# Inverting only the diagonal halves of the triangular matrices of a chunked recurrence

## The chip, the cores and the metric

The kernel runs on one core of a Trainium2 chip. The metric is the device time of one execution in microseconds. Its engines are TensorE (PE), VectorE (DVE), ScalarE (ACT), GpSimd (POOL), and SyncE (SP), which issues all of this kernel's transfers. TensorE's clock has two levels, 1.2 and 2.4 GHz; the profile gives the granted clock of a stretch as a share of the higher.

## What is computed

For 32 heads (4 batches of 8) with a state of 40x40 and 768 steps:

```python
for t in range(S):
    y[:, :, t] = einsum('bhd,bhde->bhe', rt, state)
    Sa = einsum('bhde,bhe->bhd', state, at)
    state = state * wt[:, :, None, :] - einsum('bhd,bhe->bhde', Sa, bt)
    state = state + einsum('bhd,bhe->bhde', vt, kt)
```

Its output, as 3072 tokens of 320, goes through two feed-forward nets (320 to 1536 gated, 320 to 1024 with a softmax and a norm). All is float32.

## The kernel before

**Chunks and slots.** The 768 steps are cut into 24 chunks of CH = 32. Within a chunk the vectors Sa of the 32 steps depend on each other through a triangular 32x32 matrix per head, so with T, the inverse of (identity less that matrix), all come at once: u = T rn, where rn is what the state at the chunk's start gives. Two chunks form a group n (12 groups), with 64 matrices. The work runs in slots, one for a chunk and half of the heads: `slot(s)`, s from -6 to 48; state-carrying slots are 0 to 47. The time of a slot is read here from one copy rn (line 298) to the next.

**The places of a slot.** A slot has ten places, `work`, in the order in which every engine gets its instructions (each engine runs its own in that order, and waits where it must): 0 `m_r` (matmuls pr, copy rn) and `m_st` (the state turned, pst); 1 and 2 `m_ruv` (matmuls pruv, then two masks RL on VectorE); 3 `m_u` (matmuls pu = T rn, on ScalarE four copies into Z and one us); 4 and 5 `products` of chunk half s + 9 (pABK, copies abn, a store of abn to DRAM `ab`); 6 `m_y` (pY); 7 `m_state` (pS; VectorE adds into the next Z, in two slots of four with a product with PE, line 332); 8 `m_ut` and `natural` (put, pBK). After each place `fill` puts other work in: from slot 6 on one unit of the first net on TensorE at four of the places (`UNITS`; a gate or value of 8 matmuls, or an output of 6), pieces of a weight conversion (tile `flat`, lines 584 to 603), and a share of the list `back`.

**The solve.** `back` holds the solve of group n, by forward substitution on VectorE. Partitions are the 64 matrices times two halves (even and odd rows), so that one instruction serves all. `t_iter(n, j)`, j from 0 to 30, multiplies column j of the rows so far with row j of M into `tmp` (line 260) and adds it to TT (line 264); both are split in two where VectorE is to shorten a dependence, and half of group 1 runs on GpSimd. Group n is solved in the slots s = 4n - 5 + k, k = 0 to 3 (in slots 17 and 21, k is 2), by the table `SOLVE`; in k = 0 twelve empty places come first. `decay` (two scans, lines 154 and 161, a check, line 144, a reciprocal and a copy) stands at the head of `back` in the slots of k = 2 and k = 3.

**Transfers.** `t_load` brings M (two copies, 64 rows of 4 KB each) at place 6 of the slot before k = 0, once the last store of abn has landed. `t_store` writes TT to DRAM (`tt`) in rows of 32 numbers, after k = 3; for group 0 after slot -3. `t_fetch` brings TB for a chunk at place 4 of odd slots. SP issues in the same order and waits at an instruction whose data isn't there.

**PSUM.** Four buffers go round for pr, pst, pruv, pu, pABK, pS, put and pBK.

Of the kernel before, what the change touches and what calls it, by code (L numbers as in the profile page):

```python
# [24 lines left out]
CH = 32  # L25
# [8 lines left out]
SOLVE = (0, 0, 13, 26, 31), (0, 0, 11, 21, 31), (0, 6, 15, 23, 31)  # L34
T1 = 2
STORE = 5
# [6 lines left out]
UNITS = (2, 5, 7, 9)  # L43
# [25 lines left out]
class Attention:  # L69
    def __init__(self, tc, ctx, d, xT, abd, ttd, bad, ident, zero, memory):  # L70
# [21 lines left out]
        self.tmp = [cp.tile([128, 160], F32, name=f"tmp{i}") for i in range(3)]  # L92
# [19 lines left out]
        for t in self.Z + self.UV:  # L112
            nc.gpsimd.memset(t, 0.0)
# [84 lines left out]
    def products(self, i):  # L198
# [40 lines left out]
    def eye(self, n):  # L239
        TT = self.T[n] = self.sb.tile([128, CH // 2, CH], F32, tag="TT", name=f"TT{n}", bufs=2)  # L240
        self.nc.sync.dma_start(out=TT.rearrange("p j t -> p (j t)"), in_=self.d["ceye"])
        return TT

    def t_load(self, n):
        nc = self.nc
        M = self.sb.tile([128, CH, CH], F32, tag="M", name=f"M{n}", bufs=2)
        twice(nc, M.rearrange("p j t -> p (j t)"), self.abd[n])
        self.T[n] = (M, self.T.get(n) or self.eye(n))

    def t_iter(self, n, j):  # L250

        nc = self.nc
        M, TT = self.T[n]
        k, m = CH - 1 - j, j // 2 + 1

        cut = min(m, T1) if n == 1 else m // 2 if m >= 4 and n in (0, 2) else 0
        parts = [(nc.vector, slice(0, cut), self.tmp[j % 2]), (nc.gpsimd if n == 1 else nc.vector, slice(cut, m), self.tmp[2 if n == 1 else j % 2])][cut == 0:1 + (cut < m)]

        def mult(eng, r, tmp):
            eng.tensor_tensor(out=tmp[:, 0:m * k].rearrange("p (c t) -> p c t", t=k)[:, r], in0=TT[:, r, j:j + 1].broadcast_to([128, r.stop - r.start, k]),  # L260
                              in1=M[:, j:j + 1, j + 1:CH].broadcast_to([128, r.stop - r.start, k]), op=ALU.mult)

        def add(eng, r, tmp):
            eng.tensor_tensor(out=TT[:, r, j + 1:CH], in0=TT[:, r, j + 1:CH], in1=tmp[:, 0:m * k].rearrange("p (c t) -> p c t", t=k)[:, r], op=ALU.add)  # L264
        return [lambda x=x, f=f: f(*x) for f in (mult, add) for x in parts]

    def t_store(self, n):
        M, TT = self.T.pop(n)
        for par in range(2):
            self.nc.sync.dma_start(out=self.ttd[n].rearrange("p (c two t) -> p two c t", two=2, t=CH)[:, par], in_=TT[64 * par:64 * par + 64])  # L270
# [11 lines left out]
    def t_fetch(self, c):  # L282
        n, k = divmod(c, SS)
        self.nc.sync.dma_start(out=self.TB[c % 2], in_=self.ttd[n].rearrange("(k h q) (j t) -> k (q j) h t", k=SS, q=4, t=CH)[k])

    def m_r(self, i):
# [1212 lines left out]
```

## Time and profile before

| | us |
|---|---|
| median of 3 runs | 1196.82 (1193.41 to 1199.75) |
| the profiled execution | 1195.06 |
| its span in the profile | 1193.3 |
| VectorE busy | 888.6 (74%) |
| TensorE busy (matmuls) | 1019.1 (85%) |
| ScalarE, GpSimd busy | 582.7, 484.9 |
| granted clock, mean | 0.931 |

The profile is of one execution, whose own time is 1.8 us more than its span. Busy time is an average over stages: before slot 0 (to 73 us), slots 0 to 5 with the conversion of the first net's weights (to 178.5), slots 6 to 37 (to 606.7), slots 38 to 47 (to 705.7), and the rest of the nets. Busy shares of TensorE include pipelined overlap; how far it is full is best seen where one matmul group follows the next without a gap.

### The profile page before, as it was taken

The numbers are of one execution on the slowest core, as the hardware profiler recorded it, in microseconds if no ns is written. First come the engines' busy times: TensorE is split into PE (matmuls) and PEld (weight loads), VectorE is DVE, ScalarE is ACT, GpSimd is POOL, SyncE is SP. The second block draws the span as 40 slices with busy tenths as digits, with TensorE's granted clock in tenths as the row PEclk, the third lists the DMA queues.
The fourth block names the chain that finished last, engine by engine and source line by source line (L and its number), as shares of the span: only waits on it lengthen the run. The fifth ranks groups of instructions, "written<-read, shape, count | busy, mean of one in ns | idle before, by whom it ended". The sixth has DMA issues, their size and how long they took to land.

```text
span 1193.3 us, 32044 instructions
## 1 busy us (share of the span) xinstructions
PE 1019.1 (85%) x12677; PEld 874.1 (73%) x12710; DVE 888.6 (74%) x2132; ACT 582.7 (49%) x1503; POOL 484.9 (41%) x545
## 2 busy tenths in 40 slices
PE   5536778786978888787989998999999998999997
PEld 2313547675867777676878888888888876888897
DVE  8969999999998999999999644554311249776673
ACT  4244545565656555655666754434322234454453
POOL 7548644455554546554543322222222211222232
PEclk8668977898989988998999999999999999999999
DMA  6464655566667575665655734422110000000001
GB/s 179 127 146 124 149 140 128 143 163 165 157 182 185 144 190 146 189 155 149 176 146 152 193 91 121 135 80 83 29 65 1 1 1 1 23 18 23 17 23 37
DMA packets 187951, 130.53 MB, mean 109 GB/s; under 512 B 107216, under 2 KB 167376, under 8 KB 187792
## 3 DMA queue, kind: packets, MB, share of 16 engines
q1 hardware_dynamic: 187792, 128.38, 40.8%
q8 instruction: 103, 1.69, 0.6%
q14 instruction: 56, 0.46, 0.1%
HBM read 104.19 MB, written 24.15 MB: 108 GB/s over the span
## 4 chain that ended last, share of the span: by engine, by line
PE 47%; DVE 36%; DMA 7%; issue 4%; ACT 2%; SPq 2%; POOL 2%; DVEq 0%; ACTq 0%; POOLq 0%
PE hid L816 20%; DVE tmp L260 8%; DVE TT L264 8%; DVE Z L329 3%; PE three L1182 2%; PE three L1185 2%; PE three L1183 2%; DVE RL L370 2%; DVE Q L154 2%; PE two L849 2%; PE two L1169 2%; PE two L851 2%; DVE G L161 1%; PE two L850 1%; PE one L816 1%
## 5 line engine op out<-in xcount | busy, mean ns | idle before, releaser
L264 DVE TENSOR_TENSOR TT<-TT,tmp 128x30 f32<-128x30 f32 (+38 forms) x422 | 160.6, 389 | 8.2
L816 PE MATMUL hid<-l_x,l_w 128*128 128x512 f32 x672 | 160.3, 391 | 0.0
L260 DVE TENSOR_TENSOR tmp<-TT,M 128x30 f32<-128x30 f32 (+38 forms) x422 | 148.6, 361 | 11.8 <-DMA TT<-in_ceye_dram 6.8
L816 PEld LDWEIGHTS hid<-l_x,l_w 128*128 128x128 f32 x672 | 124.4, 188 | 24.1 <-issue 0.2
L533 POOL TENSOR_TENSOR l_x<-l_plain,l_x 128x512 fp32r<-128x512 f32 x43 | 55.6, 1292 | 185.2 <-ACT l_x L532 167.7
L816 PE MATMUL one<-b_tokens,b_w 128*128 128x256 f32 x816 | 127.3, 300 | 2.3 <-DVE b_plain L837 2.3
L837 DVE TENSOR_TENSOR l_plain<-hid,l_plain 128x512 f32<-128x512 f32 x43 | 29.7, 691 | 116.2 <-ACT l_plain L836 116.1
L816 PEld LDWEIGHTS one<-b_tokens,b_w 128*128 128x128 f32 x816 | 106.6, 195 | 8.1 <-DVE b_plain L837 2.6
L223 POOL TENSOR_TENSOR AT<-abn,mA 64x256 f32<-64x256 f32 x96 | 81.7, 851 | 66.5 <-ACT abn L218 60.8
L380 PE MATMUL pY<-RL,YR 128*40 128x32 f32 x1536 | 50.8, 213 | 62.5 <-DVE RL L370 61.9
L602 POOL TENSOR_TENSOR flat<-flat 128x224 f32<-128x224 f32 (+1 forms) x54 | 38.1, 706 | 151.3 <-DVE flat L601 68.5
L380 PEld LDWEIGHTS pY<-RL,YR 128*40 128x40 f32 x1536 | 41.8, 131 | 76.4 <-DVE RL L370 72.7
L816 PE MATMUL hid<-b_w,l_x 128*128 128x512 f32 x384 | 94.0, 397 | 2.6 <-DVE l_e L1141 2.6
L532 ACT ACTIVATE b_tokens<-b_plain 128x256 fp32r<-128x256 f32 (+1 forms) x70 | 33.5, 487 | 105.5 <-DVE b_plain L837 95.7
L816 PEld LDWEIGHTS hid<-b_w,l_x 128*128 128x128 f32 x384 | 70.9, 188 | 19.0 <-DVE l_e L1141 3.6
L533 POOL TENSOR_TENSOR b_tokens<-b_plain,b_tokens 128x256 fp32r<-128x256 f32 x58 | 44.7, 770 | 91.5 <-ACT b_tokens L532 86.4
L206 PE MATMUL pABK<-AT,BK 128*64 128x64 f32 x768 | 62.1, 238 | 22.2 <-POOL BK L196 21.3
L836 ACT ACTIVATE l_plain<-hid 128x512 f32<-128x512 f32 x43 | 25.6, 597 | 110.4 <-PE hid L816 110.4
L206 PEld LDWEIGHTS pABK<-AT,BK 128*64 128x64 f32 x768 | 54.1, 150 | 33.8 <-POOL BK L196 23.5
L195 POOL TENSOR_TENSOR AT<-AT,G 40x256 f32<-40x256 f32 x90 | 70.9, 787 | 13.5 <-DMA AT<-in_LA_dram 10.3
L312 ACT ACTIVATE Z<-pu 32x160 f32<-32x160 f32 x192 | 56.3, 293 | 32.3 <-PE pu L309 29.8
L1176 POOL TENSOR_TENSOR l_w<-l_e,l_w 128x1024 fp32r<-128x1024 f32 x12 | 28.8, 2402 | 88.7 <-ACT l_e L1137 51.1
(247 smaller groups left out, 2639.9 us busy)
## 6 DMA issues: line engine op xcount, KB each, us to landing
AT<-in_LA_dram SPq DMA_DIRECT2D x48, 256.0 KB
RL<-in_RS_dram SPq DMA_DIRECT2D x24, 512.0 KB
LB<-in_LB_dram SPq DMA_DIRECT2D x46, 208.0 KB
Z<-in_VN_dram SPq DMA_DIRECT2D x48, 160.0 KB
M<-ab SPq DMA_DIRECT2D x24, 256.0 KB
UV<-in_VT_dram SPq DMA_DIRECT2D x24, 208.0 KB
G<-in_LW_dram SPq DMA_DIRECT2D x22, 214.5 KB
flat<-in_moe_w_out_dram SPq DMA_DIRECT2D x21, 224.0 KB
```

Source lines behind the costliest of these rows:

```text
L195: eng.tensor_tensor(out=at[SROW[g], g], in0=at[SROW[g], g], in1=G[SROW[g]], op=ALU.mult)
L206: yield lambda m=m: nc.tensor.matmul(ps[0:64, m * 64:m * 64 + 64], lhsT=bkt[:, m].rearrange("p s t -> p (s t)"), rhs=at[:, :, m, :], start ...
L223: nc.gpsimd.tensor_tensor(out=at[UROW[g], g].rearrange("p (a b) t -> p a b t", a=2), in0=abn[UROW[g], :, hs], in1=self.mA[UROW[g]].unsquee ...
L260: eng.tensor_tensor(out=tmp[:, 0:m * k].rearrange("p (c t) -> p c t", t=k)[:, r], in0=TT[:, r, j:j + 1].broadcast_to([128, r.stop - r.star ...
L264: eng.tensor_tensor(out=TT[:, r, j + 1:CH], in0=TT[:, r, j + 1:CH], in1=tmp[:, 0:m * k].rearrange("p (c t) -> p c t", t=k)[:, r], op=ALU.add)
L312: nc.scalar.activation(z[32 * q:32 * q + 32, hs, g, p * 4:p * 4 + 4, :], ps[32 * q:32 * q + 32, 0:160].rearrange("p (h d) -> p h d", d=40) ...
L329: nc.vector.tensor_tensor(out=o, in0=ps[SROW[g], 0:320].rearrange("p (n d) -> p n d", d=40), in1=z[SROW[g], hs, g], op=ALU.add)
L380: yield lambda m=m, g=g: nc.tensor.matmul(ps[SROW[g], m * CH:m * CH + CH], lhsT=yr[:, g, m, :], rhs=rl[:, hs, g, m, :], start=True, stop=True)
L532: nc.scalar.activation(h, src, AF.Copy)
L533: eng_l.tensor_tensor(out=l, in0=src, in1=h.bitcast(F32), op=ALU.subtract)
L602: lambda: self.eng.tensor_tensor(out=L, in0=L, in1=T, op=ALU.mult),
L816: nc.tensor.matmul(out, lhsT=a, rhs=b, start=n == 0, stop=n == 7)
```

## The change

VectorE inverts two 16x16 blocks of each matrix, the diagonal ones: partitions are now 64 matrices times two blocks, M is 16x16, and there are 15 steps of one multiplication and one addition, with no split and none on GpSimd. T = [[T1, 0], [corner, T2]] is never formed. Instead u comes in two passes: with the block-diagonal T, u1 = T rn; then the corner of the original matrix (LO, from `ab`) times u1's first half, plus rn, gives a new right side rm, and T rm is u. Line numbers of new code are those of the changed file.

```diff
-SOLVE = (0, 0, 13, 26, 31), (0, 0, 11, 21, 31), (0, 6, 15, 23, 31)
+HB = CH // 2
+SOLVE = (0, 5, 10, HB - 1)
-UNITS = (2, 5, 7, 9)
+UNITS = (3, 5, 7, 9)
...
     def t_load(self, n):
-        twice(nc, M.rearrange("p j t -> p (j t)"), self.abd[n])
+        for b in range(2):
+            r = slice(HB * b, HB * b + HB)
+            self.nc.sync.dma_start(out=M[64 * b:64 * b + 64], in_=self.abd[n].rearrange("m (j t) -> m j t", t=CH)[:, r, r])
...
     def t_iter(self, n, j):
-        k, m = CH - 1 - j, j // 2 + 1
...
+        k, m = HB - 1 - j, j + 1
+        D = TT[:, HB:].rearrange("p (c t) -> p c t", t=CH)
+        return [lambda: nc.vector.tensor_tensor(out=tmp, in0=D[:, 0:m, j:j + 1].broadcast_to([128, m, k]), in1=M[:, j:j + 1, j + 1:HB].broadcast_to([128, m, k]), op=ALU.mult),
+                lambda: nc.vector.tensor_tensor(out=D[:, 0:m, j + 1:HB], in0=D[:, 0:m, j + 1:HB], in1=tmp, op=ALU.add)]
...
     def t_store(self, n):
+        for b in range(2):
+            self.nc.sync.dma_start(out=self.ttd[n][:, HB * CH * b:HB * CH * (b + 1)], in_=TT[64 * b:64 * b + 64, HB - HB * b:HB - HB * b + HB * CH])
...
     def t_fetch(self, c):
+        self.nc.sync.dma_start(out=self.LO[c % 2][:, :, HB:CH], in_=steps(self.abd[n])[:, :, HB:CH])
...
+    def blocks(self, i, at):
+                self.nc.tensor.matmul(self.pr[r, at + x:at + x + 40], lhsT=self.TB[c % 2][r, hs * 4 + hh, :], rhs=self.rn[r, x:x + 40], start=True, stop=True)
+    def m_u1(self, i):
+        self.nc.scalar.activation(self.u1, self.blocks(i, 160), AF.Copy)
+    def m_u2(self, i):
+                self.nc.tensor.matmul(self.pr[32 * q:32 * q + 32, 320 + x:360 + x], lhsT=self.LO[c % 2][r, hs * 4 + hh, :], rhs=self.u1[r, x:x + 40], start=True, stop=True)
+        self.nc.vector.tensor_tensor(out=r, in0=self.pr[:, 320:480], in1=self.rn, op=ALU.add)
     def m_u(self, i):
-        ps = self.psum(f"pu{i}")
+        ps = self.blocks(i, 0)
...
-            if k == 0:
-                back += [None] * (12 if s >= 0 else 0)
-            steps = range(*SOLVE[min(n, 3) - 1][k:k + 2])
+            back += [f for j in range(*SOLVE[k:k + 2]) for f in self.t_iter(n, j)]
...
-            lambda: run(ruv, 4),
+            lambda: (run(ruv, 4), on and self.m_u1(s)),
             lambda: run(ruv),
-            lambda: on and self.m_u(s),
+            lambda: on and self.m_u2(s),
             lambda: run(prod, 4),
-            lambda: (run(prod), late and self.scaled(pi)),
+            lambda: (on and self.m_u(s), run(prod), late and self.scaled(pi)),
...
-        if 1 < n < NSS and k == 3:
+        if solve and k == 2:
             self.t_store(n)
-        if s == -3:
+        if s == -5:
             self.t_store(0)
             self.t_fetch(0)
```

All three steps write into pr's PSUM buffer, so pu is gone and pr is held to place 5. The seeds TT of groups 0 and 1 are loaded at the beginning.

TensorE, slot 21, from pruv to the state update. Before (pu is T rn, pABK the products, `one` a unit of the net):

```order
L366 MATMUL pruv_5365<-RL_183,UV_177 64x64 x8
L816 MATMUL one<-b_tokens,b_w 128x256 x8
L309 MATMUL pu_5391<-rn_5338,TB_185 32x40 x16
L206 MATMUL pABK_5418<-AT_159,BK_171 64x64 x8
L816 MATMUL one<-b_tokens,b_w 128x256 x8
L380 MATMUL pY_187<-RL_183,YR_179 40x32 x16
L326 MATMUL pS_5472<-Z_181,YR_180 40x40 x16
```

The same stretch of the changed kernel:

```order
L385 MATMUL pruv_5758<-RL_183,UV_177 64x64 x4
L305 MATMUL pr_5714<-rn_5731,TB_185 32x40 x16
L385 MATMUL pruv_5758<-RL_183,UV_177 64x64 x4
L319 MATMUL pr_5714<-u_21_5763,LO_188 32x40 x16
L831 MATMUL one<-b_tokens,b_w 128x256 x8
L207 MATMUL pABK_5824<-AT_159,BK_171 64x64 x4
L305 MATMUL pr_5714<-rm_5810,TB_185 32x40 x16
L207 MATMUL pABK_5824<-AT_159,BK_171 64x64 x4
L831 MATMUL one<-b_tokens,b_w 128x256 x8
L399 MATMUL pY_187<-RL_183,YR_180 40x32 x16
L345 MATMUL pS_5898<-Z_181,YR_180 40x40 x16
```

The one group pu has become three, each with an engine's work in between; the last of them stands between the halves of pABK.

VectorE, slot 21, from the head of the decay on (`rm` is the new right side, on which TensorE's second block product waits):

```order
L145 TENSOR_SCALAR G_0_5209<-G_0_5209 104x8x64
L155 SCALAR_TENSOR_TENSOR Q_193<-G_0_5209,d_152 104x528
L614 SCALAR_TENSOR_TENSOR flat<-flat 128x224
L159 RECIPROCAL d_152<-Q_193 104x8
L160 COPY PE_0_5710<-Q_193 104x8
L162 SCALAR_TENSOR_TENSOR G_0_5209<-G_0_5209,d_152 104x528
L389 TENSOR_TENSOR RL_183<-pruv_5758,mR 64x256 x2
L258 TENSOR_TENSOR tmp_190<-TT_4707,M_5144 128x55
L259 TENSOR_TENSOR TT_4707<-TT_4707,tmp_190 128x11x5
L321 TENSOR_TENSOR rm_5810<-pr_5714,rn_5731 128x160
```

The addition for rm is new; it stands behind the whole decay and the masks, where in the kernel before the masks RL were the last on which TensorE (pY) waited.

SP, around the store of T(0), of the changed kernel; before, it stood two slots later, behind the loads of UV and RL:

```order
L265 DMA tt_86<-TT_334 64x512 x2
L281 DMA TB_185<-tt_86 128x8x32
L282 DMA LO_188<-ab_74 128x8x16
L167 DMA AT_160<-in_LA_dram 128x512
L173 DMA LB_465<-in_LB_dram 104x512
L221 DMA ab_75<-abn_450 32x8x32 x4
```

The store, which waits for the solve, and the fetch behind it now come ahead of the loads of AT and LB and of a store of abn.

## Rows read from the trace of the kernel before

**Rows 1.** Stages (windows): us from:to, length, busy (instructions) per engine, PEclk, DMA share, GB/s.

```profile
73.00:178.50 105.50, 74.95 (x1155) 46.89 (x1171) 93.57 (x248) 50.01 (x149) 66.73 (x99) 0.84 0.57 143
178.50:606.70 428.20, 349.70 (x6702) 310.15 (x6714) 407.87 (x1002) 248.99 (x747) 227.68 (x275) 0.92 0.64 164
606.70:705.70 99.00, 94.21 (x1949) 84.82 (x1952) 75.19 (x219) 65.35 (x201) 33.69 (x49) 1.00 0.52 139
```

**Rows 2.** The same windows, instructions on the solve's tile tmp alone.

```profile
73.00:178.50 105.50, 39.76 (x131) 24.18 (x54) 0.84 0.57 143
178.50:606.70 428.20, 209.66 (x522) 0.00 (x0) 0.92 0.64 164
```

**Rows 3.** Windows of slots 15, 17 and 19, columns as in rows 1.

```profile
302.50:312.70 10.20, 10.16 (x215) 9.29 (x215) 9.06 (x26) 6.73 (x22) 5.76 (x8) 1.00 0.70 169
325.40:341.30 15.90, 12.69 (x221) 11.15 (x221) 15.48 (x32) 9.37 (x27) 13.21 (x14) 0.85 0.84 226
353.00:367.60 14.60, 12.12 (x231) 11.04 (x231) 11.64 (x35) 6.83 (x23) 5.48 (x8) 0.88 0.92 224
```

**Rows 4.** VectorE groups, 178.5 to 606.7: busy us, mean ns | idle before.

```profile
L329 DVE TENSOR_TENSOR Z<-pS,Z 40x320 f32<-40x320 f32 x64 | 31.0, 485 | 0.4
L370 DVE TENSOR_TENSOR RL<-pruv,mR 64x256 f32<-64x256 f32 x64 | 26.7, 418 | 2.0
L154 DVE TENSOR_TENSOR_SCAN Q<-G,d 104x528 f32<-104x528 f32 x15 | 25.2, 1680 | 0.5
L161 DVE TENSOR_TENSOR_SCAN G<-G,d 104x528 f32<-104x528 f32 x15 | 21.1, 1410 | 0.0
L332 DVE TENSOR_TENSOR Z<-Z,PE 40x320 f32<-40x320 f32 x32 | 19.2, 601 | 1.1
L597 DVE SCALAR_TENSOR_TENSOR flat<-flat 128x224 int32<-128x224 int32 x38 | 16.5, 435 | 2.4 <-ACT flat L584 2.1
...
L144 DVE TENSOR_SCALAR G<-G 104x512 f32<-104x512 f32 x15 | 7.0, 465 | 0.0
```

**Rows 5.** Timeline, slots 22 and 23: start us, us, engine, line, instruction.

```profile
404.17 0.23 DVE L260 TENSOR_TENSOR tmp<-TT,M 128x78 f32<-128x78 f32 x1
...
409.58 0.67 POOL L602 TENSOR_TENSOR flat<-flat 128x224 f32<-128x224 f32 x1 [3.23 <-DVE flat L601]
409.65 0.65 DVE L260 TENSOR_TENSOR tmp<-TT,M 128x30 f32<-128x30 f32 x1
...
410.33 0.19 DVE L264 TENSOR_TENSOR TT<-TT,tmp 128x30 f32<-128x30 f32 x1
```

**Rows 6.** Timeline of TensorE in slot 27.

```profile
467.37 0.49 PE L309 MATMUL pu<-rn,TB 32*32 32x40 f32 x32
467.79 1.15 PE L206 MATMUL pABK<-AT,BK 128*64 128x64 f32 x16
468.86 0.42 PE L849 MATMUL two<-b_w,b_tokens 128*128 128x320 f32 x1
...
469.94 0.81 PE L380 MATMUL pY<-RL,YR 128*40 128x32 f32 x32
470.68 0.81 PE L326 MATMUL pS<-Z,YR 64*40 64x40 f32 x32
471.41 1.20 PE L816 MATMUL one<-b_tokens,b_w 128*128 128x256 f32 x8
```

**Rows 7.** ScalarE groups, 178.5 to 606.7, the copy rn.

```profile
L298 ACT ACTIVATE rn<-pr 128x160 f32<-128x160 f32 x33 | 10.0, 302 | 0.8 <-PE pr L295 0.2
```

**Rows 8.** The chain that ended last, 606 to 626: start us, us, what.

```profile
613.87 2.75 DMA ab<-abn
...
617.21 4.80 DMA M<-ab
```

**Rows 9.** The same chain, 55 to 75.

```profile
59.97 2.93 DMA tt<-TT
```

**Rows 10.** Timeline of GpSimd, 22 to 78; in brackets its idle time before.

```profile
70.36 1.50 POOL L223 TENSOR_TENSOR AT<-abn,mA 64x256 f32<-64x256 f32 x2 [22.16 <-ACT abn L218]
```

More of the change, by code (lines that the diff above doesn't have):

```diff
@@ L111, in __init__ @@
             nc.vector.memset(t, 0.0)
-        for t in self.Z + self.UV:
+        for t in self.Z + self.UV + self.LO:
             nc.gpsimd.memset(t, 0.0)
@@ L253, in t_iter @@
         M, TT = self.T[n]
-        k, m = CH - 1 - j, j // 2 + 1
[L256 to L265, printed above, removed]
+        k, m = HB - 1 - j, j + 1
+        D = TT[:, HB:].rearrange("p (c t) -> p c t", t=CH)
+        tmp = self.tmp[j % 2][:, 0:m * k].rearrange("p (c t) -> p c t", t=k)
+        return [lambda: nc.vector.tensor_tensor(out=tmp, in0=D[:, 0:m, j:j + 1].broadcast_to([128, m, k]), in1=M[:, j:j + 1, j + 1:HB].broadcast_to([128, m, k]), op=ALU.mult),
+                lambda: nc.vector.tensor_tensor(out=D[:, 0:m, j + 1:HB], in0=D[:, 0:m, j + 1:HB], in1=tmp, op=ALU.add)]
     def t_store(self, n):
         M, TT = self.T.pop(n)
-        for par in range(2):
-            self.nc.sync.dma_start(out=self.ttd[n].rearrange("p (c two t) -> p two c t", two=2, t=CH)[:, par], in_=TT[64 * par:64 * par + 64])
+        for b in range(2):
+            self.nc.sync.dma_start(out=self.ttd[n][:, HB * CH * b:HB * CH * (b + 1)], in_=TT[64 * b:64 * b + 64, HB - HB * b:HB - HB * b + HB * CH])
     def z_load(self, c):
@@ L421, in begin @@
                 self.eye(0)
+                self.eye(1)
             run(self.products(i))
@@ L437, in slot @@
         n, k = divmod(s - (2 * SS + 1 - LOOK), 2 * SS)
-        if 0 < n < NSS:
-            if k == 0:
-                back += [None] * (12 if s >= 0 else 0)
+        solve = 0 < n < NSS and k < 3
+        if solve:
             if k == 2 and n + 1 < NSS:
                 self.eye(n + 1)
-            steps = range(*SOLVE[min(n, 3) - 1][k:k + 2])
-            back += [f for j in steps for f in self.t_iter(n, j)]
-        if s in range(-6, -2):
-            back += [f for j in range((s + 6) * 8, min((s + 7) * 8, CH - 1)) for f in self.t_iter(0, j)]
+            back += [f for j in range(*SOLVE[k:k + 2]) for f in self.t_iter(n, j)]
+        if s in (-6, -5):
+            back += [f for j in range((s + 6) * 8, min((s + 7) * 8, HB - 1)) for f in self.t_iter(0, j)]
         m, hs = pi // (2 * SS) + 1, (pi % (2 * SS)) // 2
@@ L475, in slot @@
                 self.t_load(pj // (2 * SS))
-            if s == 3 and p == STORE:
-                self.t_store(1)
             if p == 4 and s % 2 and 3 < s < NHS - 1:
```

52 lines of the change are left out of this document (30 added, 22 removed).

## The prediction

> **What bounds the kernel now.** I read the stages first, then VectorE alone, then single slots. By stage [rows 1] the last 488 us, the feed-forward part, hold nothing that the diff touches, so I let them stand. In slots 6 to 37 (178.5 to 606.7 us, 32 slots of 13.38 us) VectorE is busy 407.9 of 428.2 us, 95%, TensorE 349.7. Of VectorE's time 209.7 us are the triangular solve: 522 instructions of 0.40 us [rows 2]. So VectorE sets the pace, and half of its work there is what the change cuts. The single slots [rows 3] show the other limit: where few solve instructions fall (slot 15, from 302.5), TensorE is busy 10.16 of 10.2 us at full clock. In slot 17 (from 325.4), which also has a decay, VectorE is busy 15.48 of 15.9 us and TensorE's clock is 0.85.
>
> **The solve.** For one n there were 31 steps of a multiplication and an addition, two instructions each or, split, more: 522/8 = 65 per n in this stage. Now it is 15 steps, 30 instructions. The elements per partition fall from 2856 to 680 (the sum of rows times remaining columns over the steps), so from 92 a step to 45. The time of one instruction hardly depends on that: undisturbed it is 0.23 us at 78 elements and 0.19 at 30 [rows 5]. The 0.65 us at 409.65 is a wait: GpSimd's instruction runs from 409.58 to 410.25, VectorE's ends at 410.30. I take 0.40 less the 0.04 that the shorter work saves, 0.36 us; the bounds are 0.19 (never held up) and 0.65 (always). The Trainium skill, SBUF — State Buffer, section Who interferes with whom, says that an instruction of VectorE with two SBUF inputs and one of GpSimd that reads SBUF exclude each other for a whole instruction. Rows 5 agree to 0.05 us. By that rule the saving goes with the count of instructions, 65 to 30; were it to go with the elements, one would cost 0.40 x 45/92 = 0.20 us and the 30 would cost 6 us and not 10.8. So per four slots VectorE drops from 209.7/8 = 26.2 to 10.8 us, plus four additions for r. Such an addition (128x160, one input in PSUM) is not in the trace: at least 0.19, and I take the 0.42 of the mask RL (64x256 from PSUM) [rows 4]. VectorE's work per slot: (407.9 - 209.7)/32 + 10.8/4 + 0.42 = 9.3 us.
>
> **TensorE.** Two groups of 16 matmuls come in per slot, shaped like pu. From one start to the next, pu took 467.79 - 467.37 = 0.42 us [rows 6], so 0.84 us a slot. LO has half the rows; I don't credit that. Floor: 10.2 + 0.84 = 11.0 us, above VectorE's 9.3. So TensorE would set the pace wherever nothing else holds it up.
>
> **The new waits.** The step to u is now PE, ACT, PE, DVE, PE. The activation u1 costs 0.30 us, as rn does [rows 7]; on TensorE half of pruv, about 0.5 us, lies between it and the corner, so I cost it at nothing. ScalarE, busy 249 of 428 us [rows 1], has room for 0.3 more; if its queue holds another copy there, TensorE stands about as long. The addition for r is the dear one. It stands on VectorE behind everything from the state update Z on, and TensorE's second block product stands before pY and pS, on which the next Z waits. That is a loop: VectorE from Z to r, then TensorE from the block product to pS. TensorE's part by [rows 6]: pu 0.42, half of pABK 0.53, a unit 1.08, pY 0.74, pS 0.73, together 3.5; I add 0.2 for hand-overs.
> - Slots with a decay and a solve (k = 2): Z 2 x 0.49, RL 2 x 0.42, scans 1.68 and 1.41, check 0.47 [rows 4], five solve instructions 1.8, four pieces of some 0.43 (as L597), two tiny ones at 0.19, r 0.42: 9.7. Loop 13.4 us.
> - k = 3, a decay and the solve's last two instructions: about 8.0 by the same prices (one scan, two solve instructions, seven pieces), loop 11.7.
> - k = 1: Z with PE 4 instructions 2.2, six solve instructions 2.2, three pieces, RL, r: 6.9, loop 10.6, under the floor. k = 0 is shorter.
>
> So four slots take 11.0 + 11.0 + 13.4 + 11.7 = 47.1 us in place of 4 x 13.38 = 53.5, **51 us less over slots 6 to 37**.
>
> **M.** The 12 empty places ahead of the first step of each n go, and M is now wanted at once. In the trace the store of abn takes 2.75 us to land and M another 4.80 [rows 8]; from the store's last issue to M's landing it is 617.21 + 4.80 - 613.87 = 8.1 us, some 9 from the copies of abn. Against that stand some 6 us of TensorE's work to the next slot's first place (three units, pY, pS, the short groups [rows 6]), and VectorE runs another 1 to 2 behind. So VectorE stands 2 to 3 us there, in a k = 0 slot whose loop has over 2 us to spare: I cost it at nothing, and the cover is just that spare time. M's pieces become 64 B, 2048 of them in place of 128 of 4 KB. The nearest row, the store of T in 2048 pieces of 128 B, landed in 2.93 us [rows 9], so I expect no longer landing. The Trainium skill, DMA: Bandwidth & Descriptors, section Specifications, wants 512 B or more per piece and speaks of a read-modify-write below; the rows do not show it dearer, and it is priced among the rivals. LO adds one transfer in two slots to SP's queue, behind TB; T's store falls to 128 pieces.
>
> **The other stages.** Slots 0 to 5 (105.5 us): VectorE busy 93.6, solve 39.8 [rows 1, 2]; now 50 instructions x 0.36 + 6 x 0.42 = 20.5, so 74.3. TensorE's 75.0 + 6 x 0.84 = 80 is the larger; slot 0 keeps some 6 us of waiting for weights, and I add 2 for friction: 88, **18 less**. Ahead of slot 0, GpSimd stands 22.16 us [rows 10] since SP waits for the store of T(0); that store now comes two slots earlier in SP's order and after half as many instructions, but holds up two more slots of loads. I take **3 less**, bounds 10 less and 3 more. Slots 38 to 47 (99 us) are TensorE's already, 94.2 busy: 10 x 0.84 = 8.4 more, less about 3 where VectorE still solved, and some 1.5 in each of the last two, where no unit covers the hand-overs: **8 more**.
>
> **Sum:** -51 - 18 - 3 + 8 = -64. The profiled execution took 1195.06 us (1.8 below the median of 1196.82), so **1131 us**. The bounds: with the solve instruction at 0.20 us and no stall, slots 6 to 37 stand at TensorE's floor; at 0.65, the k = 2 loop grows by 5 x 0.29 = 1.5 us and k = 3 by 0.6, 17 us over the eight groups.
>
> **The rivals.**
> 1. *TensorE's floor everywhere.* VectorE makes up its lag across slots and the clock stays at 1.00 as in slot 15 [rows 3]: 32 x (13.38 - 11.0) = 76 saved, 20 early, 3, 6 lost late: 1195 - 93 = 1102. For it: the floor is above VectorE's mean. Against: loops do not average. 0.14.
> 2. *M late.* If its landing doubles, VectorE stands some 4.8 us longer in each k = 0 slot, half of it beyond the spare time: ten times 2.4 = 24 us back, 1155. The Trainium skill's rule on small pieces (DMA: Bandwidth & Descriptors, Specifications) would lead here. 0.14.
> 3. *Transfers set the pace.* The queues were busy 0.92 of the slot at 353.0 and 0.84 of that at 325.4 [rows 3]. If these two of every four stay at 13.4 us, four slots make 49.5: 32 us saved in place of 51: 1150. Against: over the stage four slots hold 428.2 x 0.64 / 8 = 34 us of transfers [rows 1], under 47. 0.13.
> 4. *Slower: the wait for r in every slot.* The price of the new place on VectorE decides. If its list from Z to r takes over 9.7 us in all slots, not in one of four, the loop passes 13.4. That needs solve instructions near 0.9 us, above anything but the worst. Then slots 14 us: +20, late +8, early -5: 1218. 0.05.
> 5. *No change*: what VectorE saves returns as other waits of TensorE, 1195. 0.04.
>
> **How the numbers follow.** The forecast, 1112 to 1148, gets 0.5; rivals 2 and 3 lie above it, rival 1 below. Leaving out part of rival 1 and the two last, the range is 1098 to 1163. Over 0.5% (6 us, about what can be told from no change) faster: 0.5 + 0.14 + 0.14 + 0.13 = 0.91; same 0.04; slower 0.05.
>
> **What would show it.** Right: solve on VectorE about 85 us in slots 6 to 37 at 0.3 to 0.4 each; k = 0 and 1 slots near 11 us with TensorE full; the longest wait of TensorE on r, in k = 2. Wrong: VectorE standing on M by over 3 us per n, TensorE waiting for u1, slots of equal length above 12.5, or a longer feed-forward part.

## The result: slower by 1.2%, and where the time went

The changed kernel took **1211.17 us** (median of 4, 1206.81 to 1212.65) beside 1196.53 for the kernel before (1193.41 to 1199.75): ratio 1.0116, 95% interval 1.0078 to 1.0154. The forecast was 1131, the range 1098 to 1163. The profiled execution took 1212.65 us, its span is 1210.7.

**The profile after, by stage** (windows from one slot's first copy rn to another's: slots 0 to 5, 6 to 37, 38 to 47; columns as in [rows 1], which these answer to):

```profile
68.50:172.90 104.40, 73.10 (x1529) 47.30 (x1550) 84.36 (x194) 51.67 (x156) 39.95 (x44) 0.90 0.52 126
172.90:613.30 440.40, 380.99 (x8774) 335.24 (x8786) 307.13 (x753) 256.25 (x778) 228.35 (x276) 0.91 0.61 156
613.30:719.00 105.70, 100.30 (x2551) 89.11 (x2554) 60.12 (x177) 66.46 (x209) 31.91 (x48) 1.00 0.50 133
```

Of these windows the tile tmp alone, VectorE's columns, as in [rows 2]:

```profile
68.50:172.90 104.40, 19.86 (x59) 0.90 0.52 126
172.90:613.30 440.40, 85.81 (x239) 0.91 0.61 156
```

VectorE did get rid of the work: the solve fell from 209.66 to 85.81 us, VectorE's busy time in slots 6 to 37 from 407.87 to 307.13. Yet the stage became 12 us longer. VectorE is now busy 70% of it, TensorE 87%. The chain that ended last says the same. First the kernel before, then the changed one (the page's shares of the span by engine):

```profile
PE 47%; DVE 36%; DMA 7%; issue 4%; ACT 2%; SPq 2%; POOL 2%; DVEq 0%; ACTq 0%; POOLq 0%
```

```profile
PE 59%; DVE 12%; DMA 10%; ACT 8%; SPq 6%; issue 4%; POOL 1%; ACTq 0%; DVEq 0%; POOLq 0%
```

What VectorE lost on the chain went to TensorE, but also to ScalarE, DMA and SyncE's queue: work and hand-overs that were hidden before. Where they stand, the waits tell. Of the kernel before in slots 6 to 37 (engine, line, what it waited for: us in all, times, longest):

```profile
POOL AT L223 <- ACT abn L218: 19.3, 13, 5.6
...
ACT Z L312 <- PE pu L309: 17.9, 16, 3.0
```

Of the changed kernel, the same stage:

```profile
ACT Z L331 <- PE pr L305: 98.0, 29, 5.2
POOL AT L223 <- ACT abn L218: 97.6, 32, 8.1
DVE yt L403 <- PE pY L399: 34.4, 18, 3.5
PE pr L305 <- DVE rm L321: 30.1, 21, 3.5
DVE tmp L258 <- DMA M<-ab: 19.4, 7, 3.9
```

ScalarE stands 98.0 us at u's copies (before 17.9), GpSimd 97.6 us for abn (before 19.3), and TensorE 30.1 us for r. Of the three only the last is a wait of TensorE, which is now the busiest engine; whether the other two cost time, the experiments tell. From the starts of the copies rn (line 297, before 298), the mean slot of each kind, eight of each in slots 6 to 37, is in us:

| | k = 0 | k = 1 | k = 2 | k = 3 |
|---|---|---|---|---|
| before | 11.62 | 13.46 | 15.21 | 13.25 |
| forecast | 11.0 | 11.0 | 13.4 | 11.7 |
| after | 14.14 | 11.97 | 15.09 | 13.85 |

The slots with k = 1 gained 1.5 us; those with k = 0, in which M is wanted, lost 2.5.

**Slot 31, a k = 0 slot of 17.46 us.** VectorE's timeline (start us, us, engine, line, instruction, in brackets the idle time before):

```profile
516.87 1.26 DVE L614 SCALAR_TENSOR_TENSOR flat<-flat 128x224 f32<-128x224 f32 x1
522.01 0.17 DVE L258 TENSOR_TENSOR tmp<-TT,M 128x15 f32<-128x15 f32 x1 [3.88 <-DMA M<-ab]
...
523.72 0.31 DVE L321 TENSOR_TENSOR rm<-pr,rn 128x160 f32<-128x160 f32 x1
```

TensorE's, the same stretch:

```profile
519.89 0.68 PE L207 MATMUL pABK<-AT,BK 128*64 128x64 f32 x8
524.08 0.75 PE L305 MATMUL pr<-rm,TB 32*32 32x40 f32 x32 [3.52 <-DVE rm L321]
```

And in windows of 4 us (columns as in [rows 1]; the clock is the third number from the end):

```profile
518.00:522.00 4.00, 2.57 (x55) 2.17 (x53) 0.13 (x1) 1.19 (x4) 0.00 (x0) 1.00 0.89 213
522.00:526.00 4.00, 1.92 (x41) 1.71 (x42) 3.51 (x14) 1.05 (x4) 1.22 (x2) 0.66 0.99 244
526.00:530.00 4.00, 4.00 (x70) 3.61 (x70) 0.54 (x2) 1.49 (x5) 2.14 (x3) 0.50 0.63 138
530.00:534.00 4.00, 4.00 (x80) 3.67 (x75) 2.47 (x7) 2.10 (x7) 1.11 (x2) 0.99 0.96 274
```

The first tmp of the solve stands 3.88 us for M, which has not landed. VectorE works in order, so the two masks RL and r wait behind it. TensorE works in order too, so the second half of pABK, which needs nothing from r, waits 3.52 us behind the second block product. Then the granted clock is at its lower level (0.50, 1.2 GHz) all through the window from 526, although TensorE is full again, and comes back in the one from 530. The block product takes 0.75 us where it took 0.49 [rows 6]. Of the r waits that the timeline shows, 14 us fall in k = 0 slots and 12 in k = 2 slots.

**Why M is late.** The chain of waits across slots 17 and 18 (start us, us, what):

```profile
333.55 6.14 DMA b_plain<-xT
...
339.80 0.84 ACT b_tokens L547
...
342.41 0.71 ACT Q L138 x2
...
343.15 0.81 ACT Q L138 x2
...
343.99 0.31 ACT rn L297
...
344.34 0.75 PE pr L305 x32
...
349.88 0.73 PE pr L305 x32
350.64 0.29 ACT Z L331
...
351.89 0.30 ACT us L333
352.21 0.38 ACT abn L218
...
354.38 3.23 DMA ab<-abn
...
358.38 2.90 DMA M<-ab
```

Before, u's product stood at place 3, ahead of pABK, and waited for nothing on VectorE. Now it stands at place 5 ahead of pABK's second half, and on ScalarE abn's copies come behind five copies of u. The store of ab, M's load and GpSimd's products all start from abn. Here M lands at 358.38 + 2.90 = 361.28, 9.1 us after abn's first copy. That abn's place behind u is what makes M late, and that late M is what costs, is so far only an argument; kernel 1 below tests it.

### The profile page after: what moved, and what is told of

Its sections match the earlier page's. It is cut to its first block, busy times and chain, and to the rows that moved or that the text cites. A ratio compares the mean times of both kernels' runs of the same rounds, so it can differ in the third digit from the quotient of the medians.

```text
span 1210.7 us, 37943 instructions
## 1 busy us (share of the span) xinstructions
PE 1058.3 (87%) x15743; PEld 907.3 (75%) x15782; DVE 744.1 (61%) x1696; ACT 593.6 (49%) x1551; POOL 461.5 (38%) x493
## 4 chain that ended last, share of the span: by engine, by line
PE 59%; DVE 12%; DMA 10%; ACT 8%; SPq 6%; issue 4%; POOL 1%; ACTq 0%; DVEq 0%; POOLq 0%
PE hid L831 20%; PE one L831 5%; DMA b_plain<-xT 3%; PE pr L305 3%; PE pABK L207 2%; PE two L864 2%; PE three L1197 2%; PE three L1200 2%; PE three L1198 2%; DMA M<-ab 2%; PE pY L399 2%; PE two L866 2%; PE pruv L385 2%; PE two L865 2%; PE pS L345 2%
## 5 line engine op out<-in xcount | busy, mean ns | idle before, releaser
L223 POOL TENSOR_TENSOR AT<-abn,mA 64x256 f32<-64x256 f32 x96 | 74.0, 771 | 156.9 <-ACT abn L218 152.9
L331 ACT ACTIVATE Z<-pr 32x160 f32<-32x160 f32 x192 | 56.5, 295 | 141.2 <-PE pr L305 129.8
L207 PE MATMUL pABK<-AT,BK 128*64 128x64 f32 x768 | 75.8, 255 | 37.1 <-POOL BK L197 35.5
L207 PEld LDWEIGHTS pABK<-AT,BK 128*64 128x64 f32 x768 | 62.5, 163 | 52.2 <-POOL BK L197 36.9
L831 PEld LDWEIGHTS hid<-b_w,l_x 128*128 128x128 f32 x384 | 72.1, 191 | 19.3 <-DVE l_e L1156 3.6
L196 POOL TENSOR_TENSOR AT<-AT,G 40x256 f32<-40x256 f32 x90 | 78.0, 867 | 19.2 <-DMA AT<-in_LA_dram 16.0
L258 DVE TENSOR_TENSOR tmp<-TT,M 128x15 f32<-128x15 f32 (+4 forms) x180 | 59.4, 330 | 35.3 <-DMA M<-ab 30.2
L385 PE MATMUL pruv<-RL,UV 128*64 128x64 f32 x768 | 67.8, 234 | 6.9 <-ACT YR L236 6.3
L385 PEld LDWEIGHTS pruv<-RL,UV 128*64 128x64 f32 x768 | 54.3, 143 | 17.8 <-ACT YR L236 8.3
L259 DVE TENSOR_TENSOR TT<-TT,tmp 128x15 f32<-128x15 f32 (+4 forms) x180 | 65.8, 366 | 2.7
L305 PE MATMUL pr<-rm,TB 32*32 32x40 f32 x1536 | 26.5, 214 | 42.9 <-DVE rm L321 41.8
```

The source lines that it names most:

```text
L196: eng.tensor_tensor(out=at[SROW[g], g], in0=at[SROW[g], g], in1=G[SROW[g]], op=ALU.mult)
L207: yield lambda m=m: nc.tensor.matmul(ps[0:64, m * 64:m * 64 + 64], lhsT=bkt[:, m].rearrange("p s t -> p (s t)"), rhs=at[:, :, m, :], start ...
L223: nc.gpsimd.tensor_tensor(out=at[UROW[g], g].rearrange("p (a b) t -> p a b t", a=2), in0=abn[UROW[g], :, hs], in1=self.mA[UROW[g]].unsquee ...
L258: return [lambda: nc.vector.tensor_tensor(out=tmp, in0=D[:, 0:m, j:j + 1].broadcast_to([128, m, k]), in1=M[:, j:j + 1, j + 1:HB].broadcast ...
L259: lambda: nc.vector.tensor_tensor(out=D[:, 0:m, j + 1:HB], in0=D[:, 0:m, j + 1:HB], in1=tmp, op=ALU.add)]
L305: self.nc.tensor.matmul(self.pr[r, at + x:at + x + 40], lhsT=self.TB[c % 2][r, hs * 4 + hh, :], rhs=self.rn[r, x:x + 40], start=True, stop ...
```

## The experiments

Each kernel was timed in rounds with the kernel before on the same chip; its medians lay between 1194.95 and 1197.63. Theory A, B and C in the first four texts: A, TensorE's wait for r, which the two-pass chain brings; B, M's landing after the 12 empty places are gone; C, abn and the store of ab made late by u's place.

**1. The halved solve alone,** with u in one pass at place 3, `UNITS` as before the change and no transfer of LO:

```diff
-            lambda: (run(ruv, 4), on and self.m_u1(s)),
+            lambda: run(ruv, 4),
...
-            lambda: on and self.m_u2(s),
+            lambda: on and self.m_u(s),
...
-            lambda: (on and self.m_u(s), run(prod), late and self.scaled(pi)),
+            lambda: (run(prod), late and self.scaled(pi)),
```

> The halved solve alone: u is one pass with the block-diagonal T, at place 3 as before; the corner is left out of the computation. Theory A (the two extra passes give the gain back): without them the saving on VectorE shows, slots 6 to 37 near TensorE's floor of 10.2 to 11.5 us, total 1100 to 1125. Theory B (M wanted too early and its wait throttles TensorE): M is as late as in the changed kernel, slots of k = 0 stay near 14 us, total 1165 to 1185. Theory C (the copies of abn stand behind u's copies on ScalarE, so store, M and GpSimd are late): u's copies come before abn's here too, but early; total 1120 to 1150.

**2. The chain alone,** with before's whole solve: `t_iter`, `t_store` and `t_fetch` as before, `m_u1`, `m_u2`, `m_u` and the places as in the change, a corner of zeros.

> The two passes alone: the whole 32x32 solve of the kernel before, the corner tile all zero, so that the second pass repeats the first. Theory A: slots lengthen by the waits of the path, 1.5 us or more each, total 1250 to 1280. Theories B and C: VectorE carries 0.42 us more per slot and TensorE 0.84, of which VectorE's counts, total 1210 to 1230.

**3. The empty places back.**

```diff
+            if k == 0 and s >= 0:
+                back += [None] * 12
```

> The changed kernel with the 12 empty places put back ahead of the first step of each n. Theory B: VectorE no longer stands on M (19 us in slots 6 to 37), nor TensorE behind it at half clock; k = 0 slots fall from 14.1 to about 11.5 us, total 1180 to 1190. Theories A and C: the wait moves to r, total 1205 to 1212.

**4. The products first.**

```diff
-            lambda: (on and self.m_u(s), run(prod), late and self.scaled(pi)),
+            lambda: (run(prod), on and self.m_u(s), late and self.scaled(pi)),
```

> The changed kernel with the second block product behind all of pABK at place 5, so that the copies of abn stand before u's copies on ScalarE. Theory C: abn is stored and M lands over 2 us sooner, GpSimd no longer stands 98 us on abn, total 1180 to 1195. Theory A: the path to u is 0.5 us longer and nothing else, total 1210 to 1220. Theory B: as C, if M is the point.

| kernel | us | ratio to before, 95% |
|---|---|---|
| 1 halved solve alone | 1129.18 (1125.92 to 1133.38) | 0.9439 (0.9401 to 0.9477) |
| 2 chain alone | 1265.72 (1259.55 to 1271.20) | 1.0575 (1.0522 to 1.0628) |
| 3 empty places back | 1199.85 (1197.51 to 1207.30) | 1.0043 (1.0019 to 1.0066) |
| 4 products first | 1176.47 (1174.18 to 1179.02) | 0.9824 (0.9795 to 0.9854) |

The cut in the solve is worth 66 us. The chain is what costs: some 70 us more on top of a busy VectorE, 82 us between kernel 1 and the changed one. One moved call takes back 35 of these 82, the empty places 11. So the order, which theory C spoke of, has the largest single share. No theory's ranges hold throughout: kernel 1 lies in C's, kernel 2 in A's (1250 to 1280), kernel 3 between B's and those of A and C, and kernel 4 some 4 us below C's.

Kernel 1 also shows that late M alone costs little. Of its waits in slots 6 to 37:

```profile
DVE tmp L258 <- DMA M<-ab: 26.0, 8, 3.8
```

VectorE stands longer for M than in the changed kernel (19.4 us), in each of the eight k = 0 slots, and yet these take 10.85 us in the mean. There is no r in it; what TensorE wants of VectorE behind M are the masks RL and Z, for which it stands 2.7 us in these eight slots together. And abn's copies stand behind u's here too.

Kernel 4's waits in the same stage show what the order mended:

```profile
POOL AT L223 <- ACT abn L218: 38.0, 18, 6.6
...
DVE tmp L258 <- DMA M<-ab: 13.2, 6, 3.6
PE pr L305 <- DVE rm L321: 11.4, 11, 2.1
...
ACT Z L331 <- PE pr L305: 8.3, 10, 1.8
```

The k = 0 slots fall from 14.14 to 11.59 us, the k = 2 slots from 15.09 to 14.00. Kernel 3 brings k = 0 to 11.46, but the steps that it puts off make k = 1 slots 13.87.

**5 to 8. Both; the transfer's split later; r first in VectorE's queue; ScalarE's copies behind.** All but the last are made on kernel 4: the empty places of kernel 3; `self.ready` at place 1 of the next slot; no shared-out work before place 3 (`if p > 2 or s < 6 else 0` behind the share). Number 8 is the change, with `m_u` cut in two by a `yield` behind `self.blocks(i, 0)`:

```diff
-            lambda: (on and self.m_u(s), run(prod), late and self.scaled(pi)),
+            lambda: (on and next(mu), run(prod), on and next(mu, None), late and self.scaled(pi)),
```

> The last kernel (second block product behind the pABK products) plus the 12 empty places ahead of the solve's first step. Run apart, the order took 1211.2 to 1176.5 and the places took 1211.2 to 1199.9 (11 us). Theory C (both cure the same thing: abn and the store of ab come late because they stand behind u): with the order mended the places are worth at most 4 us more, 1172 to 1180. Theory M (the late M is a cost of its own, VectorE standing still for it): the gains add, 1162 to 1168. In the trace of the order alone VectorE's tmp still waits 13.2 us for M in slots 6 to 37, in 6 places.

> The second block product behind the pABK products, and ScalarE's and VectorE's split of the loaded xT (line 547 and 548) written one place into the next slot instead of at place 7 of the slot that loads it. Theory X (in one slot of four ScalarE stands at line 547 until xT has landed, 6.4 us after its issue; UV, YR and rn stand behind it, TensorE idles some 3 us and then runs at 0.50 of its clock for 6 us in the next slot): slots of k=2 fall from 14.0 to about 12 and of k=3 from 13.6 to about 11.5, 8 of each, so some 30 us less: 1140 to 1155. Rival (the wait only moves to the gate matmuls that use the split tokens, at place 3 of the next slot): 1168 to 1180.

> The second block product behind the pABK products, and in slots from 6 on none of VectorE's solve steps, decays and pieces of conversion of the list that is shared out stands before place 3, where r is added. Theory R (r comes late because VectorE's queue is long at place 3, and TensorE idles for it: 11.4 us in slots 6 to 37, and loses clock behind it): the second block product waits under 3 us in all, 1155 to 1168. Rival (the wait is small beside what the same work costs when it is crowded into seven places, and the solve then ends later): 1174 to 1190.

> The changed kernel, with the order on TensorE as it is there (the second block product ahead of the second half of pABK), but ScalarE's five copies of u behind the copies of abn. It tells which queue makes abn late. Theory S (ScalarE: abn's copies stand behind the copies of u): 1175 to 1185, as with the whole product moved. Theory T (TensorE: the second half of pABK stands behind a product that waits for r): 1200 to 1212.

| kernel | us | ratio to before, 95% |
|---|---|---|
| 5 order and empty places | 1179.14 (1166.34 to 1182.93) | 0.9823 (0.9753 to 0.9894) |
| 6 split of xT later | 1187.78 (1185.90 to 1193.33) | 0.9935 (0.9908 to 0.9961) |
| 7 r first on VectorE | 1177.32 (1175.90 to 1179.25) | 0.9833 (0.9803 to 0.9863) |
| 8 u's copies behind abn's | 1193.09 (1189.36 to 1196.44) | 0.9960 (0.9942 to 0.9977) |

Number 5: with the order mended the empty places bring no gain that these runs can tell (one of the four took 1166.34, the others 1178.55 to 1182.93). That fits theory C, but not that M was late because abn was: in kernel 4 VectorE still stands 13.2 us for M, while TensorE stands 0.9 us in all for r in the k = 0 slots. Number 6 misses both of its ranges: slots 6 to 37 take 405.8 us as against 405.6, and slots 38 to 47 became 8 us longer. Number 7 took TensorE's wait for r away and gained nothing; its own waits of TensorE, slots 6 to 37:

```profile
PE pst L374 <- DVE Z L348: 13.3, 12, 2.4
PE pr L305 <- ACT rn L297: 7.9, 8, 1.2
```

The 11.4 us returned one step later, at the state Z, since the work was only moved behind r. Number 8 falls between both theories: ScalarE's order alone gives 18.1 of the 34.7 us.

**9 to 12. TensorE's time alone, and three variants.** Number 9 is kernel 1 with two more block products behind u's that nobody reads:

```diff
         ps = self.blocks(i, 0)
+        for at in (160, 320):
+            self.blocks(i, at)
```

Number 10 is kernel 4 with `UNITS = (2, 5, 7, 9)`. Number 11 is kernel 4 with `self.load(b + 1)` at the last place of the slot before. Number 12 is kernel 2 with the order of kernel 4.

> The kernel with the halved solve and u in one pass (it leaves the corner out, 1129.2), plus two more block products of 16 matmuls behind u's own in each slot, whose results nobody reads: the chain's TensorE time without its two evictions, its wait for r or its order. Theory P (of the 47 us between that kernel and the changed one with its products first, TensorE's own time is nearly all: in slots 6 to 37 TensorE is busy 366.4 us against 336.8): 1162 to 1175. Theory Q (the waits for u1 and r are the larger part): 1135 to 1155.

> The second block product behind the pABK products, with the first filler matmuls of a slot at place 2 again, as before the change (UNITS 2 in place of 3): ahead of the corner product in place of behind it. Theory F (the filler behind the corner product covers VectorE's addition of r; without it the second block product or pABK's second half comes up against it): pABK's eight matmuls of place 4 still stand between, so about 0.3 to 0.8 us a slot more, 1185 to 1200. Rival (pABK covers r alone, and the filler now covers u1's copy): 1165 to 1178.

> The second block product behind the pABK products, with the load of xT (line 870) issued one place earlier on SyncE: at the end of the slot before, ahead of that slot's loads of G, AT and LB, which stood in front of it. The transfer took 5.1 to 6.4 us from issue in the chain of waits, with the DMA engines at full share. Theory X2 (ScalarE at line 547 waits for that transfer, and the clock falls behind the stall): it lands 2 to 3 us earlier in 7 slots, and the clock's fall goes with it where the stall goes: 1150 to 1165. Rival (another wait of the same two slots takes its place, as when the split was put later): 1170 to 1185.

> The kernel with before's whole solve and the two-pass chain on top (corner of zeros, 1265.7), with the second block product behind the pABK products. With the halved solve that order was worth 35 us. Theory C (the cost is abn's place behind u, whatever VectorE does): 35 us here too, 1225 to 1238. Rival V (with VectorE setting the pace the chain costs by its wait for r, an addition at the end of a queue that never empties, and the order matters little): 1245 to 1266. Were TensorE's own time all that is left of the chain, VectorE's longer slots would hide it: 1200 to 1215.

| kernel | us | ratio to before, 95% |
|---|---|---|
| 9 idle products | 1155.03 (1147.69 to 1159.33) | 0.9645 (0.9597 to 0.9693) |
| 10 filler at place 2 | 1173.31 (1170.04 to 1178.52) | 0.9794 (0.9771 to 0.9817) |
| 11 xT's load a place earlier | 1170.41 (1167.20 to 1172.95) | 0.9770 (0.9746 to 0.9794) |
| 12 chain alone, products first | 1236.11 (1232.69 to 1237.07) | 1.0319 (1.0295 to 1.0342) |

Number 9 lies at the upper edge of what theory Q gave. TensorE's time costs some 26 us (25.9 between the medians; number 9's interval is 6 us to either side), and 21 are left for the chain's evictions, waits and place. Not all of the 26 need be TensorE's own: the idle products write into the tile that u's copies read, and ScalarE stands 42.4 us at these copies where it stood 23.5 in kernel 1. The windows of slots 6 to 37 of kernels 1, 9 and 4 (columns as in [rows 1]):

```profile
167.36:545.20 377.84, 336.82 (x6709) 300.21 (x6722) 308.89 (x719) 249.40 (x747) 238.77 (x275) 0.94 0.70 179
```

```profile
167.81:562.67 394.86, 352.78 (x8776) 316.76 (x8785) 310.49 (x720) 250.00 (x746) 231.55 (x276) 0.95 0.67 173
```

```profile
172.67:578.25 405.58, 366.38 (x8774) 325.23 (x8786) 309.48 (x753) 254.58 (x779) 232.38 (x276) 0.94 0.67 170
```

The idle products add 16 us of TensorE's busy time and 17 to the stage, so hardly any of it is hidden. Number 12 puts the order's worth at 30 us where VectorE is nearly full as well (415 of 455 us). Its 39 us over before go together with the wait that rival 4 of the prediction spoke of, though no run takes it away there; of TensorE's waits in slots 6 to 37:

```profile
PE pr L309 <- DVE rm L325: 49.9, 21, 4.6
```

Number 10 makes no clear difference. Number 11 gives 6 us, less than theory X2 expected: the k = 2 slots fall from 14.00 to 13.29, those of k = 3 from 13.59 to 12.90.

**13 to 18. Which wait.** Numbers 13 and 14 are kernel 4, 15 is the change; 16 joins 4, 10 and 11.

```diff
-rhs=self.u1[r, x:x + 40]
+rhs=self.rn[r, x:x + 40]
```

is number 13. In 14 and 15 the line `self.rn = r` is left out. In 17 (the change) and 18 (kernel 4) it is left out too, and the addition reads no PSUM:

```diff
-        self.nc.vector.tensor_tensor(out=r, in0=self.pr[:, 320:480], in1=self.rn, op=ALU.add)
-        self.rn = r
+        self.nc.vector.tensor_tensor(out=r, in0=self.rn, in1=self.rn, op=ALU.add)
```

> The second block product behind the pABK products; the corner product reads rn in place of u1, so that it no longer waits for ScalarE's copy of u1, which is still made (the corner is applied to other numbers than it should be). Of the 21 us between this order (1176.5) and the kernel with as many idle products (1155.0), it tells u1's share. Theory R (r's wait is the rest): 1172 to 1180. Theory U1 (the corner's wait is): 1155 to 1165.

> The second block product behind the pABK products; the second block product reads rn in place of r, so that it waits for no addition on VectorE, which is still made (the corner is left out of the result). Theory R: in slots 6 to 37 the second product stands 11.4 us for r; without that and the clock lost behind it 1155 to 1165. Theory U1: 1172 to 1180.

> The changed kernel with its own order (second block product ahead of the second half of pABK), where that product reads rn in place of r (the corner is left out of the result). Putting ScalarE's copies of u behind abn's alone gave 18 of the 35 us that the whole order is worth. Theory T (the other half is pABK's second half standing behind a product that waits for r): without that wait 1172 to 1190, half or more of the 35 us. Rival (abn behind u's five copies costs the same whether r is waited for or not): 1193 to 1208.

> The three edits that took time off one by one, together: second block product behind the pABK products (1176.5), the load of xT one place earlier (1170.4), the first filler at place 2 (1173.3). If they add: 1167. If the filler's gain was chance (its interval touches that of the order alone): 1170.

> In the last two kernels that read rn in place of r the trace still shows the second block product waiting for VectorE's addition (33.5 and 11.5 us in slots 6 to 37), since that addition reads the PSUM tile that the product writes. Here the addition reads rn twice, from SBUF, and the second product reads rn, so that this wait is gone; the order is that of the change (product ahead of the second half of pABK), and the corner is left out of the result. Theory T (half of the 35 us that the order costs is pABK's second half behind a product that waits for r): 1172 to 1195. Rival (abn behind u's five copies costs all of it, whether r is waited for or not): 1200 to 1222.

> The same two edits with the products first (1176.5 with the wait). Theory R (of the 21 us between that kernel and the one with idle products at 1155.0, the wait for r and the clock lost behind it are most): 1155 to 1167. Rival (u is two places later in the slot than in the kernel with idle products, and u1's copy is one more on ScalarE; the wait for r costs nothing): 1172 to 1180.

| kernel | us | ratio to before, 95% |
|---|---|---|
| 13 corner reads rn | 1177.31 (1175.09 to 1178.19) | 0.9842 (0.9806 to 0.9878) |
| 14 product reads rn, products first | 1179.48 (1176.75 to 1182.77) | 0.9872 (0.9833 to 0.9910) |
| 15 product reads rn, the change's order | 1220.90 (1219.34 to 1221.98) | 1.0207 (1.0171 to 1.0243) |
| 16 three edits | 1173.58 (1172.16 to 1176.26) | 0.9820 (0.9785 to 0.9856) |
| 17 no wait for r, the change's order | 1191.20 (1190.22 to 1193.37) | 0.9953 (0.9938 to 0.9967) |
| 18 no wait for r, products first | 1171.53 (1170.50 to 1174.30) | 0.9798 (0.9763 to 0.9832) |

Numbers 13, 14 and 15 tell nothing of their waits, since these were still there. TensorE's waits in slots 6 to 37, of number 13 and then of number 14:

```profile
PE pr L319 <- ACT u L311: 5.4, 1, 5.4
```

```profile
PE pr L305 <- DVE rm L321: 11.5, 12, 2.2
```

In kernel 4 the first is 5.4 us in one place as well. The copy of u1 and the addition read the PSUM tile that the products write, and the products wait for that too. So what the wait for u1 is worth stays untested; in slots 6 to 37 the trace of kernel 4 shows TensorE idle for it in that one place. (Why number 15 is even 10 us slower than the change stays open.) In 17 and 18 the wait is gone. In 17 the line of TensorE for r is missing from the waits, while VectorE stands for M as long as before:

```profile
DVE tmp L258 <- DMA M<-ab: 20.4, 7, 4.1
```

M is as late, nobody waits for r, and 20.0 us come back. They come back where M is wanted: the k = 0 slots fall from 14.14 to 11.63 us, those of k = 2 stay (15.09 and 15.07), although TensorE had stood 12 us for r there. So M's late landing costs time through r behind it. With the products first the same edit gives 5.0 between the medians; the two intervals of the ratio overlap, and theory R's 1155 to 1167 is not reached. The shares of order and wait overlap: the order alone takes off 34.7, the wait alone 20.0, both together 39.6. The three edits together (16) do not add, and lie outside both of their forecasts; the lowest median of a kernel that leaves nothing out is number 11's, 1170.41 us, 2.3% under before. The halved solve is worth having, with the second block product behind pABK.

## Why the prediction was wrong

The terms of the sum, in us, beside the profiled executions:

| | forecast | measured |
|---|---|---|
| slots 6 to 37 | -51 | +12.2 |
| slots 0 to 5 | -18 | -1.1 |
| ahead of slot 0 | -3 | -4.5 |
| slots 38 to 47 | +8 | +6.7 |
| the rest of the nets | 0 | +4.1 |

The third and fourth were right. (Where slot 47 ends is read to about 1 us, so the last two rows are best taken together: +8 forecast, +10.8 measured.) Why the nets took 4.1 us longer no run shows.

- **The solve on VectorE: right.** 85 us were forecast, 85.81 measured, an instruction at 0.36 us (85.81 / 239). VectorE stopped being the bound.
- **TensorE's 0.84 us a slot: right in kind, too dear.** 48 slots make 40 us; number 9 measured 25.9. (Its idle products are both of 32 rows, where LO has 16, so it is no exact copy.)
- **The new waits: the step that failed.** I asked of each wait whether other work covered it, but not what stands behind the waiting instruction. On VectorE r stands behind the first tmp of the solve, which waits for M; on TensorE the half of pABK that needs nothing from r stands behind the product that waits for it; on ScalarE abn's two copies stand behind five copies that wait for that product. "ScalarE has room" was said of u1's copy alone, from a busy share of 249 of 428 us; it is the order that decides. For all this the sum had the k = 2 and k = 3 loops, 2.4 and 0.7 us a slot above the floor, and nothing in k = 0, where 14.14 us were measured and not 11.0. The gap between number 9 and the change is 56 us. ScalarE's order is 18.1 of it (number 8), the rest of the order 16.6 (number 4), the wait for r that then remains 5.0 (number 18). Taken the other way round, the wait for r is 20.0 and the order behind it 19.7.
- **The last 16.5 us of the gap** are not separated: u two places later in the slot, u1's copy, r's addition, LO's transfer, `UNITS`. The traces say where they fall: number 18's k = 3 slots take 14.08 us where number 9's take 11.82, and its other kinds are no longer than number 9's. In these slots the first block product waits for rn, a wait that neither the forecast nor an experiment looked at (number 18, TensorE's waits in slots 6 to 37):

```profile
PE pr L305 <- ACT rn L297: 8.7, 9, 1.2
```

  In the chain across slots 17 and 18 rn stands behind four copies Q on ScalarE, and TensorE has only pst and half of pruv between pr, which rn copies, and that product. The mean granted clock of number 18's k = 3 slots is 0.77, of number 9's 0.86. That this is the cause is not shown.
- **M costed at nothing: right for M alone, wrong with r behind it.** VectorE stood 19.4 us in 7 places, 2.8 in the mean, where I had 2 to 3, and 9.1 us passed from abn's first copy to M's landing, where I had some 9. Kernel 1, with 26.0 us of the same standing and no r, has k = 0 slots of 10.85 us. What failed is that the k = 0 loop, Z to r to pS, was taken to have over 2 us to spare for it: with r behind M the slot took 14.14, without the wait for r 11.63. Rival 2 had the place but not the cause: M's landing did not double (2.90 us in the chain above, 5.02 in one of kernel 1's, 4.80 before [rows 8]).
- **r priced at 0.42 and u1 at 0.30:** these groups took, in slots 6 to 37 (busy us, mean ns | idle before):

```profile
L321 DVE TENSOR_TENSOR rm<-pr,rn 128x160 f32<-128x160 f32 x32 | 9.9, 309 | 0.0
```

```profile
L311 ACT ACTIVATE u<-pr 128x160 f32<-128x160 f32 x32 | 9.7, 302 | 4.2 <-PE pr L305 3.5
```

  Neither price was too low; their places were what cost.
- **The floor and slots 0 to 5: too low, the second step that failed.** Take the chain's 40 us out of the sum and the halved solve alone stands at 1091; it took 1129.18. The floor of 10.2 us is there: eight of kernel 1's slots 6 to 37 take 9.76 to 10.16. But its means are 10.85, 10.95, 14.44 and 10.99. So the k = 2 slot is long without any r, and that the 13.4 us of its loop came near was luck. In kernel 1 TensorE stands 12.7 us for UV and 14.3 us for Z in slots 6 to 37. UV stands behind ScalarE's line 547, which waits for the transfer of xT (6.14 us in the chain above, with UV, YR and rn behind it; rival 3 had the transfers, at 1150). How much of the slot the transfer sets is not shown: issued a place earlier (number 11) it gave 0.7 us of it. In slots 0 to 5 the solve gave back 19.9 us, nearly as forecast (39.76 to 19.86), but VectorE's busy time fell by only 9.2, and kernel 1's stage by 6.4, where I had 18, or 23 without the chain's 5. Conversions that had stood elsewhere came in, 8.3 us more of them on VectorE in the changed kernel, 7 of one kind for 5. The kernel before, then the changed one, VectorE's groups in that stage:

```profile
L602 DVE TENSOR_TENSOR b_plain<-b_plain 128x384 f32<-128x384 f32 (+1 forms) x5 | 2.9, 584 | 0.0
```

```profile
L617 DVE TENSOR_TENSOR b_plain<-b_plain 128x384 f32<-128x384 f32 (+1 forms) x7 | 3.8, 536 | 0.2
```

- **The sum of the misses:** 1129.2 - 1091 = 38 for what the cut brings, 25.9 - 40 = -14 for TensorE's time, 56 for queues and waits: 80, which is 1211 - 1131. The 1091 still hold the loops' 25 us, which are the forecast's own price for waits; counted there, the misses are about 63, -14 and 31. So what limits the slots once the solve is short was misjudged by at least as much as the waits.
- **Rival 4, slower:** it gave 1218, near the result, and its mechanism, TensorE held up by r, is 20.0 us of it (number 17). But its condition, a long VectorE list in every slot, did not come about: r comes late behind M and in the k = 2 slots. Where it is made to (numbers 2 and 12), TensorE waits 59.6 and 49.9 us for r.

## What to carry to other kernels

When a step is cut in two and moved, list for every engine what now stands behind the moved instructions and what that work starts: here two copies of 0.38 us behind u fed a store, a load, GpSimd and the next solve. Late data costs where something that the busiest engine waits for stands behind the wait: the late M cost little in kernel 1, and 20 us with r behind it. A busy share says whether an engine has time, not whether it has it at that place in its order. Try the order before giving up the idea: one exchanged call was worth 35 us, and turned a loss of 1.2% into a gain of 1.8%.

## What the runs showed of the hardware

- A stall of 3.52 us cost TensorE more than itself: the granted clock was 0.50 all through the window from 526 to 530, in which TensorE was full, and the slot took 17.46 us. Number 17's slots of its kind, with the same order and no such wait, take 11.63 in the mean.
- M, 128 KB, came in 2048 pieces of 64 B and landed in 2.90 us; before, it was 512 KB in 128 pieces of 4 KB and took 4.80 [rows 8]. In kernel 1's chain one load of the small pieces took longer:

```profile
327.49 5.02 DMA M<-ab
```

  So a quarter of the bytes in sixteen times as many pieces landed sooner in one chain and about as late in the other. No run compares the two piece sizes with the same bytes.
- A matmul group that writes one part of a PSUM tile waited for an engine that read another part of it: in number 14, where the product no longer used r, TensorE's wait for the addition stayed at 11.5 us, and in number 18, where the addition read no PSUM, it was gone. No run tells whether the program or the chip asks for that wait.
